# The second channel product of an attention and mixer kernel: its first block product is copied between PSUM banks by ScalarE, and the products come in another order

## The chip, the core and the metric

The kernel runs on one core of a Trainium2 chip. The metric is the device time of one execution in microseconds (us). Every time below is in us unless it is marked ns.

## What is computed

Eight batches of a gated attention unit without softmax, and behind it a token and channel mixer. All sizes are fixed: 3008 rows, 256 columns, 64 columns of `z`, 256 hidden token columns, 1536 hidden channel columns.

```python
scores = (z @ z.T) / 3008                 # per batch, 3008 x 3008
attn   = maximum(scores, 0) ** 2
x      = u * (attn @ v)                   # 3008 x 256
h      = maximum(x.T @ w_tok1, 0) @ w_tok2
u2     = x + h.T
h2     = maximum(u2 @ w_ch1, 0) @ w_ch2   # first and second channel product
out    = u2 + h2
```

The change is in the second channel product, `maximum(u2 @ w_ch1, 0) @ w_ch2`, alone.

## The kernel before

Work is tiled by blocks of 512 rows, six for each batch (`q` = 0 to 5; the last has 448). For each batch `b`, attention blocks come first; then the mixer of that batch: the first token product (`tok1`, L1058, tile `a_ps`), the second (`tok2`, L1128, tile `h_ps`), and for each block `q` the first channel product in six chunks (`ch1`, four matmuls of L1192 into tile `hp`, then a relu by ScalarE at L1231 into `h2pre`) and the second.

The second channel product uses a Strassen-like scheme with seven block products in place of eight. The hidden activations of a block of rows are seen as a 2 x 2 matrix of quarters (halves of the rows, even and odd hidden tiles), and so are the weights `w_ch2`. VectorE makes four sums of the quarters (`make_sums`, L1383, L1388, L1401, tile `hsum`), and mixes the weights once (`w_mix_sb`). A block product `k` is twelve matmuls of 128 columns (`product`, L1447; six where `q` = 5). After each product VectorE adds the 256 columns in PSUM to the output tile `ro` in SBUF (`collect` and its `add`, L1480; 128 columns where `q` = 5). Products that use the same sum go on accumulating in the same bank without being cleared: 1, then 6, 7 and 4 in the first bank of the tile `xb`; 5, then 3 in a bank of the tile `zb`; and product 2 alone in the other bank of `zb`. Products 1 and 2 belong to the same block of the output (columns 0 to 127 of the first half of the rows). So seven adds were needed for each `q`.

PSUM has eight banks; the kernel uses them as four pairs, or slots (`take_slot`, `bank_pair`). `xb`, `zb`, each `hp` chunk, the group tile `gp`, the attention accumulators and scores each take one while they live.

For `b` > 0 and `q` = 1 to 3 the first two of the six chunks are done in another scheme as four stages, written "a" to "d" (`grouped_ch1`, L1312, tile `gp`). Between the stages ScalarE copies one bank of `gp` to the other (`fork`, L1320) so that two accumulations can go on from one partial sum; it also copies a bank to SBUF (L1323), and takes the relus L1327 and L1331. VectorE adds two of the results at L1338.

The order of instructions on each engine is set when the program is built: a planner keeps a time for each engine, takes pieces off two lists (`heads` for token products, `tails` for channel products) when what they need is done by its own estimates, and gives the evacuations to the engines by priority (`first`). The order of pieces within `tails` is written by hand: `PLAIN` (before: a tuple without a name), `GROUPED` and `ORDER_LAST`, where a number is a block product, 0 stands for a `ch1` chunk of the next block (or, in `ORDER_LAST`, for what is left of `q` = 5 in the plain way, `ch2`, L1544) and a letter for a stage of `grouped_ch1` of the next block. There are 47 sets of seven products: every `(b, q)` but the very last, which is done by `ch2` alone. Of them 19 are in `PLAIN` order, 21 in `GROUPED` order, and 7, with `q` = 5, in `ORDER_LAST` order. The mixer of a batch and its attention do not mix piece by piece: the program has long stretches of one and of the other by turns, and the first token product of the next batch falls among the products of `q` = 5.

VectorE also makes the sums for the token product (`x_sums`, L926), the sums `t_sums` (L1268, L1273, L1278) for `grouped_ch1`, and gates and adds for attention. ScalarE does the relu of the scores (L496, L508) and copies accumulators (L825).

Of the kernel before, what the change touches and what calls it, by code (L numbers as in the profile page):

```python
# [14 lines left out]
P = 128  # L15
# [43 lines left out]
def kernel(  # L59
# [11 lines left out]
    nc = tc.nc  # L71
# [10 lines left out]
    NQ = (S + QW - 1) // QW  # L82
# [9 lines left out]
    first = ctx.enter_context(ExitStack())  # L92
# [276 lines left out]
    def push(engine, ready, busy, lat, fn, first=0, room=(), done=None, frees=()):  # L369
        op = Op(ready, busy, lat, fn, first, room, done, frees)  # L370
        waiting[engine].append(op)
        return op.done
# [577 lines left out]
    mix_done, tok_mix_done = Done(), Done()  # L950
# [70 lines left out]

    hid_done = Done()
    BORROW = 3
    GROUPED = ("a", 0, 1, 2, "b", 6, 5, 0, "c", 7, 3, 0, 4, "d")
    VERY_LAST = (B - 1, NQ - 1, CHT // 2 - 1)
    ORDER_LAST = ((1, 2, 6, 5, 7, 0, 3, 4), (1, 2, 6, 5, 0, 7, 3, 0, 4))

    def add_mixer(b):
        st = {}
# [141 lines left out]
        def with_u(q, ready, fn):  # L1171

            turned = st["turned", q].t
            if turned is None:
                st.setdefault(("waits", q), []).append(lambda t: fn(max(ready, t)))
            else:
                fn(max(ready, turned))
# [177 lines left out]
        def pairs_of(q):  # L1355

            return 2 if q < NQ - 1 else 1
# [56 lines left out]

        def bank_of(q, k):

            if k in (2, 5, 3):
                return st["zb", q][:, int(k != 2)]
            return st["xb", q][:, 0]

        def product(q, k, end):


            n = pairs_of(q)
            if k == 1:
                st["x_slot", q], _ = take_slot()
                st["xb", q] = bank_pair(st["x_slot", q], "xb")
            if k == 2:
                st["z_slot", q], _ = take_slot()
                st["zb", q] = bank_pair(st["z_slot", q], "zb")  # L1430
            to = bank_of(q, k)
            raw = {1: (0, 0), 2: (1, 0), 3: (1, 1)}
            mixed = {5: 0, 7: 1, 6: 2, 4: 3}
            w2 = w_ch2_sb.rearrange("p (j r) (h d) -> p j r h d", r=2, d=P)
            weights = {1: w2[:, :, 0, 0, :], 2: w2[:, :, 1, 0, :], 4: w2[:, :, 1, 1, :],
                       3: w_mix_sb[:, 3], 5: w_mix_sb[:, 0], 6: w_mix_sb[:, 1],
                       7: w_mix_sb[:, 2]}[k]
            first_use = k in (1, 2, 5)
            for c2 in range(CHT // 2):
                d, j = divmod(c2, 2)  # L1440
                for i in range(n):
                    if k in raw:
                        r, m = raw[k]
                        lhs = quarters(q, d)[:, r, m, j, i * P:(i + 1) * P]
                    else:
                        lhs = st["sum", q, d][:, mixed[k], j, i * P:(i + 1) * P]
                    nc.tensor.matmul(  # L1447
                        to[:, i * P:(i + 1) * P], lhs, weights[:, c2, :],
                        start=(first_use and c2 == 0 and i == 0), stop=(c2 == CHT // 2 - 1),
                        skip_group_check=True)  # L1450
            if k == 4:
                done_with_h2(q)
                for d in range(CHT // 4):
                    release(home_of(q), [1], end + 0.2)
            collect(q, k, end)

        def collect(q, k, end):


            n = pairs_of(q)  # L1460
            busy = 0.34 if n == 2 else 0.21
            source = bank_of(q, k)[:, :n * P].rearrange("p (i d) -> p i d", d=P)

            def res(m, h):
                return st["res", q][:, m * n:m * n + n, h * P:(h + 1) * P]

            def us(m, h):
                return st["u", q][:, h, m * n:m * n + n, :]

            blocks_of = {1: (0, 0), 2: (0, 0), 5: (1, 1), 6: (1, 0), 3: (1, 0), 7: (1, 1),  # L1470
                         4: (0, 1)}
            opening = k in (1, 5, 6, 4)

            def add(t):
                if k == 1:
                    home, n_home = take_home(q)
                    st["res", q] = sb.tile([P, QW // P, D], F32, tag=home, name="ro",
                                           bufs=n_home)
                m, h = blocks_of[k]
                nc.vector.tensor_add(  # L1480
                    res(m, h), source, us(m, h) if opening else res(m, h))
                recent[0] = st["res", q][:, 0, :1]
                over[q] -= 1
                if not over[q]:
                    nc.sync.dma_start(
                        out=rows_of(out[b], q)[:, :2 * n, :], in_=st["res", q][:, :2 * n, :])
                    free["sp"] = max(free["sp"], t) + 0.4
                    release(home_of(q), [1], t + 4.0)
                    release("us", us_uses[q])

            ready = end + 0.21
            done = taken[q, k]
            if k == 1:
                with_u(q, ready, lambda at: push(
                    "dve", at, busy, busy + 0.15, add, first=1, room=(home_of(q),),
                    frees=frees_of(q), done=done))
            else:
                done = push("dve", ready, busy, busy + 0.15, add, first=1, done=taken[q, k],
                            room=lambda: ("res", q) in st)
            if k == 3:  # L1500
                ring.append((done, st["z_slot", q]))
            if k == 4:
                ring.append((done, st["x_slot", q]))

        over = [7] * NQ
        us_uses = [[1] for _ in range(NQ)]
        s_done = {(q, d, k): Done() for q in range(NQ) for d in range(CHT // 4) for k in range(4)}
        taken = {(q, k): Done() for q in range(NQ) for k in range(1, 8)}
# [86 lines left out]
        for q in range(NQ):  # L1595
            heads.append(Piece(0.784, [x_done[b, NQ - 1], xd_done[b, q], tok_mix_done],
                               lambda end, q=q: tok1(q, end),
                               opens=q < NQ - 1, closes=q > 0, key=(b, 0), joins=q == 0 and b > 0))
        for q in range(NQ):
            heads.append(Piece(4 * column_time(widths[q]), [a_done[0], Sooner(a_done[1], 0.21), tok2_done[q]],  # L1600
                               lambda end, q=q: tok2(q, end), key=(b, 1)))
# [39 lines left out]
        def add_product(q, k):  # L1641
            needs = {
                1: [Sooner(h2_done[q, c], 0.111 * c) for c in range(CHT // 2)] + w_done[2:],
                2: [], 5: [mix_done, taken[q, 2]], 6: [taken[q, 1]], 3: [taken[q, 5]], 7: [taken[q, 6]],
                4: [taken[q, 7]]}[k]
            kind = {5: 0, 7: 1, 6: 2, 4: 3}.get(k)
            if kind is not None:
                needs = needs + [Sooner(s_done[q, d, kind], 0.222 * d) for d in range(CHT // 4)]
            if q == NQ - 1 and k == 5 and b % 2 == 0:
                needs = needs + [tok1_over[b + 1]]  # L1650
            cost = pairs_of(q) * (CHT // 2) * column_time(P)
            tails.append(Piece(cost, needs, lambda end: product(q, k, end), opens=k == 1,
                               closes=k == 4, key=(b, 2 + q), slot=k in (1, 2),
                               joins=k == 1 and q == NQ - 1))

        added = [0] * (NQ + 1)
# [6 lines left out]
        for q in range(NQ):  # L1663
            while added[q] < CHT // 2:
                add_next(q, q)
            if q + 1 < NQ and grouped(q + 1):
                added[q + 1] = 2
            rest = [(half, i) for half in halves(q) for i in range(pieces_of(q, half))]
            if fast(q):
                us_uses[q][0] += bool(rest)  # L1670
                h2_uses[q] += bool(rest)
                for k in (ORDER_LAST[b % 2] if q == NQ - 1 else GROUPED if grouped(q + 1) else
                          (0, 0, 1, 2, 0, 6, 5, 0, 7, 3, 0, 4)):
                    if isinstance(k, str):
                        add_grouped(q + 1, 0, "abcd".index(k), q)
                    elif k:
                        add_product(q, k)
                    elif rest:
                        add_ch2(q, *rest.pop(0))
                    elif b or q != HALF - 1 or added[q + 1] < BORROW:  # L1680
                        add_next(q + 1, q)
            else:
                for _ in range(2):
                    add_next(q + 1, q)
                for half, i in rest:
                    add_ch2(q, half, i)
# [259 lines left out]
    while cur[0] is not None or heads or tails:  # L1946
        run_engines(pe[0])
        ask_some()
        t = pe[0]
# [15 lines left out]
        n = can_score(done_units, most)  # L1965
        if n and blk is not None and blk.b == 1:
            b, q, _ = units[done_units][0]
            if b * NQ + q > NQ + blk.q + 1:
                n = 0
            if (b, q, blk.q) == (1, HALF, HALF - 1):  # L1970
                n = min(n, sum(u[0][:2] == (b, q) for u in units[:done_units]) < 2 * AHEAD)
# [118 lines left out]
```

## Time and profile before

| What | us |
|---|---|
| Three runs, median (lowest to highest) | 1109.5 (1109.03 to 1110.85) |
| The profiled execution | 1109.13 |
| Its span, first to last instruction | 1107.3 |

Busy time of the engines in the profiled execution:

| Engine | us | share of the span | instructions |
|---|---|---|---|
| PE (TensorE, matmuls) | 1102.2 | 100% | 11199 |
| PEld (weight loads) | 695.2 | 63% | 11199 |
| DVE (VectorE) | 811.5 | 73% | 1791 |
| ACT (ScalarE) | 684.7 | 62% | 906 |
| POOL (GpSimd) | 168.2 | 15% | 386 |

How to read it: an instruction row of the order in time has its start from the beginning of the span, the time it took (for several merged ones, from the first's start to the last's end), the engine, the line of the kernel, the operation, output tile and inputs, sizes, how many, and in brackets for how long the engine had been idle before and what ended that. A row of the groups has busy time, the mean of one in ns, and the idle time before. Matmuls overlap, so that the time each took says less than the distance of their starts. Line numbers are those of the kernel before.

### The profile page before, as it was taken

What the parts mean: (1) busy time and instruction counts of PE and PEld (TensorE: products, weight loads), DVE (VectorE), ACT (ScalarE), POOL (GpSimd) and SP (SyncE); (2) the same over time, 40 slices, a digit from 0 to 9 for tenths busy, and PEclk for the clock granted to TensorE, in tenths of its full rate; (3) what the DMA queues carried; (4) which work ended last, traced back from release to release, by engine and by line L of the source; (5) the groups of instructions that cost most, each with busy time, mean ns of one, the idle gap of its engine ahead of it and who ended that gap; (6) DMA issues with size and microseconds to landing.
All of it is one profiled execution on the core that took longest, in us unless ns stands there. A gap on an engine that the chain in (4) does not pass through costs nothing.

```text
span 1107.3 us, 27459 instructions
## 1 busy us (share of the span) xinstructions
PE 1102.2 (100%) x11199; PEld 695.2 (63%) x11199; DVE 811.5 (73%) x1791; ACT 684.7 (62%) x906; POOL 168.2 (15%) x386
## 2 busy tenths in 40 slices
PE   9999999999999999999999999999999999999998
PEld 3444575776557665576656865557755677556776
DVE  6889865886758866578766796567966778656785
ACT  7999555646854567546665467663776537743464
POOL 5320110321003110032100320003210120000100
PEclk9999999999999999999999999999999999999999
DMA  9999947798978969789896796977989778684222
GB/s 179 167 199 184 149 96 152 127 179 146 190 127 149 190 133 177 127 156 191 140 189 120 133 218 141 170 122 150 198 160 169 116 145 185 125 160 104 64 59 96
DMA packets 465726, 165.55 MB, mean 150 GB/s; under 512 B 433024, under 2 KB 448960, under 8 KB 465600
## 3 DMA queue, kind: packets, MB, share of 16 engines
q1 hardware_dynamic: 436208, 131.11, 58.9%
q0 software_dynamic: 28880, 32.32, 21.5%
q8 instruction: 87, 1.43, 0.6%
q14 instruction: 39, 0.32, 0.1%
q10 hardware_dynamic: 512, 0.38, 0.1%
HBM read 65.40 MB, written 24.64 MB: 81 GB/s over the span
## 4 chain that ended last, share of the span: by engine, by line
PE 99%; DVE 0%; ACT 0%; issue 0%
PE acc L697 42%; PE hp L1192 19%; PE xb L1447 11%; PE zb L1447 8%; PE sc L470 6%; PE h_ps L1128 4%; PE a_ps L1058 3%; PE gp L1312 3%; PE op L1544 2%; PE first_acc L614 1%; PE wp L210 0%; DVE at L516 0%; ACT at L508 0%; DVE zr L183 0%; PE first_acc L189 0%; DVE zT L1850 0%
## 5 line engine op out<-in xcount | busy, mean ns | idle before, releaser
L697 PEld LDWEIGHTS <-v_sb 64*128 64x128 bf16 x4418 | 245.7, 94 | 212.5 <-issue 1.3
L1231 ACT ACTIVATE h2pre<-hp 128x1024 bf16<-128x1024 f32 (+1 forms) x245 | 239.9, 1005 | 182.7 <-PE hp L1192 180.5
L697 PE MATMUL acc<-at,v_sb 64*128 64x512 bf16 (+1 forms) x2738 | 341.6, 374 | 0.0
L508 ACT ACTIVATE at<-sc 128x1024 bf16<-128x1024 f32 (+1 forms) x290 | 286.8, 1027 | 72.0 <-PE sc L470 66.4
L516 DVE TENSOR_TENSOR at<-at 128x1024 bf16<-128x1024 bf16 (+1 forms) x290 | 198.1, 687 | 112.1 <-ACT at L508 107.9
L1192 PE MATMUL hp<-xT,w_ch_sb 128*128 128x512 bf16 (+1 forms) x984 | 238.3, 374 | 0.0
L697 PE MATMUL acc<-fl,v_sb 64*128 64x512 bf16 (+1 forms) x1680 | 193.0, 367 | 0.0
L1192 PEld LDWEIGHTS <-w_ch_sb 128*128 128x128 bf16 x984 | 90.8, 98 | 79.0 <-issue 2.6
L1447 PEld LDWEIGHTS <-hsum 128*128 128x128 bf16 x2088 | 127.9, 98 | 19.6 <-issue 0.5
L470 PE MATMUL sc<-zT 64*128 64x512 bf16 (+1 forms) x732 | 132.4, 359 | 0.1
L1383 DVE TENSOR_TENSOR hsum<-h2pre 128x1024 bf16<-128x1024 bf16 (+1 forms) x141 | 90.0, 647 | 22.7 <-ACT h2pre L1231 12.6
L825 ACT COPY cp<-acc 128x512 f32<-128x512 f32 (+1 forms) x94 | 54.9, 584 | 79.9 <-PE acc L697 69.0
L831 DVE TENSOR_TENSOR cp<-acc,cp 128x512 f32<-128x512 f32 (+1 forms) x94 | 63.4, 675 | 54.8 <-ACT cp L825 54.0
L1447 PEld LDWEIGHTS <-h2pre 128*128 128x128 bf16 x1566 | 93.8, 98 | 10.0
L496 ACT ACTIVATE at<-sc 128x512 bf16<-128x512 f32 (+3 forms) x152 | 56.2, 450 | 29.2 <-PE sc L470 28.8
L1447 PE MATMUL xb<-shared_sb,hsum 128*128 128x128 bf16 x1044 | 73.6, 219 | 0.0
L1480 DVE TENSOR_TENSOR ro<-xb,u_sb 128x256 f32<-128x256 f32 (+1 forms) x141 | 56.3, 400 | 17.9 <-PE xb L1447 17.7
L470 PEld LDWEIGHTS <-zT 64*128 64x128 bf16 x732 | 42.4, 94 | 41.6 <-issue 3.8
L129 POOL CAST mark<-at 128x1 f32<-128x1 bf16 x24 | 9.3, 386 | 388.1 <-DVE at L516 388.1
L851 DVE TENSOR_TENSOR xT<-cp,uT 128x512 bf16<-128x512 f32 (+1 forms) x94 | 62.4, 663 | 0.8
L547 DVE TENSOR_TENSOR at<-at 128x512 bf16<-128x512 bf16 (+3 forms) x152 | 41.0, 320 | 23.8 <-ACT at L496 23.8
L1401 DVE TENSOR_TENSOR hsum<-h2pre,hsum 128x512 bf16<-128x512 bf16 (+1 forms) x141 | 55.1, 400 | 4.1 <-ACT h2pre L1331 2.5
(107 smaller groups left out, 1114.8 us busy)
## 6 DMA issues: line engine op xcount, KB each, us to landing
out_dram<-ro SPq DMA_DIRECT2D x40, 512.0 KB, 3.2
v_sb<-in_v_dram POOLq DMA_DIRECT2D x40, 256.0 KB, 4.6
ur<-in_u_dram POOLq DMA_DIRECT2D x40, 256.0 KB, 5.0
w_tok_sb<-in_moe_w_tok_dram POOLq DMA_DIRECT2D x10, 256.0 KB, 10.5
shared_sb<-in_z_dram POOLq DMA_DIRECT2D x35, 64.0 KB, 4.2
at<-at SPq DMA_TRANSPOSE x114, 2.4
out_dram<-ro SPq DMA_DIRECT2D x7, 256.0 KB, 3.7
fl<-at SPq DMA_TRANSPOSE x105, 4.5
```

The source lines that it names most:

```text
L470: nc.tensor.matmul(sc[:, r, c0:c1], zT[h, k:k + P], zT[h, m + c0:m + c1], start=True, stop=True)
L496: nc.scalar.activation(a3[:, i, c0:c1], sc[:, r, c0:c1], ACT.Relu, scale=inv_S)
L508: nc.scalar.activation(view, sv, ACT.Relu, scale=inv_S)
L516: nc.vector.tensor_mul(view, view, view)
L697: nc.tensor.matmul(o, vs[blk.b, g][rows, i, dh * P:(dh + 1) * P], rhs, start=(dh, h) not in blk.begun, stop=stop, skip_group_check=True)
L831: nc.vector.tensor_add(cp[:, :W], acc[:, 0, :W], cp[:, :W])
L851: nc.vector.tensor_mul(xT[:, dh, :full * P].rearrange("p (t s) -> p t s", s=P), acc[:, :full * P].rearrange("p (t s) -> p t s", s=P), uT[: ...
L1192: nc.tensor.matmul(hps[r % len(hps)][:, r, :W], w_ch1_sb[:, dc, cc * P:(cc + 1) * P], xT[:, dc, :W], start=(dc == 0), stop=(dc == DT - 1))
L1231: nc.scalar.activation(h2[:, :, :W], hp[:, :, :W], ACT.Relu)
L1383: nc.vector.tensor_sub(sums["s"][:, 0:2, :, :n * P], h[:, :, 1], h[:, 0])
L1447: nc.tensor.matmul(to[:, i * P:(i + 1) * P], lhs, weights[:, c2, :], start=(first_use and c2 == 0 and i == 0), stop=(c2 == CHT // 2 - 1), ...
L1480: nc.vector.tensor_add(res(m, h), source, us(m, h) if opening else res(m, h))
```

## The change

Product 1 is no longer added to the output by VectorE. In its place ScalarE copies its bank of `xb` (256 columns, or 128 where `q` = 5) into the second bank of `xb`, and product 2 accumulates on that copy without clearing it, while 6, 7 and 4 go on in the first bank as before. One add then takes in products 1 and 2 together. It is now the first add, the one that creates the output tile. `zb` holds only products 5 and 3, in its first bank, and its slot is taken at product 5 in place of product 2. Product 2 waits for the copy, product 6 too, and product 4 waits for product 2's add. All three orders of products change.

```diff
     BORROW = 3
-    GROUPED = ("a", 0, 1, 2, "b", 6, 5, 0, "c", 7, 3, 0, 4, "d")
+    FIRST = 2
+    GROUPED = ('a', 0, 1, 0, 'b', 6, 2, 5, 'c', 7, 0, 3, 4, 'd')
+    PLAIN = (0, 1, 0, 5, 2, 6, 0, 0, 7, 0, 3, 4)
     VERY_LAST = (B - 1, NQ - 1, CHT // 2 - 1)
-    ORDER_LAST = ((1, 2, 6, 5, 7, 0, 3, 4), (1, 2, 6, 5, 0, 7, 3, 0, 4))
+    ORDER_LAST = ((1, 2, 6, 5, 0, 7, 3, 4), (1, 2, 5, 6, 0, 3, 7, 0, 4))
...
         def bank_of(q, k):
 
-            if k in (2, 5, 3):
-                return st["zb", q][:, int(k != 2)]
-            return st["xb", q][:, 0]
+            if k in (5, 3):
+                return st["zb", q][:, 0]
+            return st["xb", q][:, int(k == 2)]
...
-            if k == 2:
+            if k == 5:
                 st["z_slot", q], _ = take_slot()
                 st["zb", q] = bank_pair(st["z_slot", q], "zb")
...
-            first_use = k in (1, 2, 5)
+            first_use = k in (1, 5)
...
-            blocks_of = {1: (0, 0), 2: (0, 0), 5: (1, 1), 6: (1, 0), 3: (1, 0), 7: (1, 1),
-                         4: (0, 1)}
-            opening = k in (1, 5, 6, 4)
+            blocks_of = {2: (0, 0), 5: (1, 1), 6: (1, 0), 3: (1, 0), 7: (1, 1), 4: (0, 1)}
+            opening = k in (2, 5, 6, 4)
+
+            def fork(t):
+                nc.scalar.copy(bank_of(q, 2)[:, :n * P], bank_of(q, 1)[:, :n * P])
 
             def add(t):
-                if k == 1:
+                if k == FIRST:
...
             if k == 1:
+                push("act", ready, busy, busy + 0.15, fork, first=2, done=done)
+            elif k == FIRST:
                 with_u(q, ready, lambda at: push(
...
-        over = [7] * NQ
+        over = [6] * NQ
...
-                2: [], 5: [mix_done, taken[q, 2]], 6: [taken[q, 1]], 3: [taken[q, 5]], 7: [taken[q, 6]],
-                4: [taken[q, 7]]}[k]
+                2: [taken[q, 1]], 5: [mix_done], 6: [taken[q, 1]], 3: [taken[q, 5]], 7: [taken[q, 6]],
+                4: [taken[q, 7], taken[q, 2]]}[k]
...
-                               closes=k == 4, key=(b, 2 + q), slot=k in (1, 2),
+                               closes=k == 4, key=(b, 2 + q), slot=k in (1, 5),
...
                 for k in (ORDER_LAST[b % 2] if q == NQ - 1 else GROUPED if grouped(q + 1) else
-                          (0, 0, 1, 2, 0, 6, 5, 0, 7, 3, 0, 4)):
+                          PLAIN):
```

## The prediction

> **What bounds the kernel now.** I read the engine table of the page first, then its chain, then the windows, then the order in time of two product sets. In the page:
>
> ```profile
> span 1107.3 us, 27459 instructions
> PE 1102.2 (100%) x11199; PEld 695.2 (63%) x11199; DVE 811.5 (73%) x1791; ACT 684.7 (62%) x906; POOL 168.2 (15%) x386
> PE 99%; DVE 0%; ACT 0%; issue 0%
> ```
>
> TensorE (PE) has something in flight during the whole span and carries 99% of the chain that ends last; VectorE (DVE) and ScalarE (ACT) have a quarter and more than a third of the span to spare. The windows say the same of the steady part and of the mixer of the last batch, the only one that no attention work of a next batch follows:
>
> ```profile
> core 0: us, PE busy (x) PEld busy (x) DVE busy (x) ACT busy (x) POOL busy (x), PEclk, DMA share, GB/s
> 40.00:1100.00 1060.00, 1059.87 (x10899) 675.18 (x10894) 780.27 (x1739) 650.98 (x869) 150.98 (x349) 1.00 0.81 149
> 1011.00:1098.00 87.00, 86.94 (x965) 64.11 (x962) 67.82 (x167) 49.46 (x60) 3.28 (x9) 1.00 0.26 66
> ```
>
> Busy TensorE is not yet TensorE at its pace, since matmuls overlap; the pace is read from starts. One set of seven products with `PLAIN` order begins so (before: a chunk of the first channel product is 4 matmuls of L1192, a block product 12 of L1447):
>
> ```profile
> 1078.43 2.75 PE L1192 MATMUL hp<-xT,w_ch_sb 128*128 128x512 bf16 x12
> 1081.02 0.83 PE L1447 MATMUL xb<-w_ch_sb,h2pre 128*128 128x128 bf16 x12
> 1081.69 0.83 PE L1447 MATMUL zb<-w_ch_sb,h2pre 128*128 128x128 bf16 x12
> 1082.36 1.03 PE L1192 MATMUL hp<-xT,w_ch_sb 128*128 128x512 bf16 x4
> 1083.22 0.83 PE L1447 MATMUL xb<-shared_sb,hsum 128*128 128x128 bf16 x12
> ```
>
> Three chunks take 2.59, so 0.86 each; a product takes 0.67, or 56 ns for a matmul of 128 columns, at a granted clock of 1.00. Each starts as the one ahead of it stops issuing. The time is therefore the matmuls' own issue time, and a change to ACT and DVE can only add waits, or take away the few that are left. One that is left shows where a wait comes from:
>
> ```profile
> 1092.02 0.92 PE L1192 MATMUL hp<-xT,w_ch_sb 128*128 128x448 bf16 x4
> 1092.97 0.83 PE L1447 MATMUL xb<-shared_sb,hsum 128*128 128x128 bf16 x12
> 1097.83 0.92 PE L1192 MATMUL hp<-xT,w_ch_sb 128*128 128x448 bf16 x4
> 1098.59 0.27 PE L1544 MATMUL op<-w_ch_sb,h2pre 128*128 128x256 bf16 x1
> 1092.50 0.42 DVE L1480 TENSOR_TENSOR ro<-xb,u_sb 128x256 f32<-128x256 f32 x1
> ```
>
> A 448-wide chunk takes 0.76 (1097.83 to 1098.59), but here product 6 (L1447, 1092.97) starts 0.95 after it: 0.2 lost, until the add of product 1 has read the bank (1092.50 + 0.42 = 1092.92). So from the end of an evacuation to the matmul that waits for it I take 0.05.
>
> **What the change removes and adds.** The built program keeps every matmul (11,200) and, between two stretches of attention, the same number of pieces of each kind; the switches between half-array and full-array work stay as many. It has 47 VectorE instructions fewer and 47 ScalarE instructions more, one for each product set (19 `PLAIN`, 21 `GROUPED`, 7 `ORDER_LAST`; 40 of 256 columns, 7 of 128). DMAs and POOL's instructions stay in number. Prices:
>
> ```profile
> L1480 DVE TENSOR_TENSOR ro<-zb,ro 128x256 f32<-128x256 f32 (+1 forms) x94 | 37.4, 398 | 3.4 <-PE zb L1447 2.7 <-POOL mark L129 0.3
> L1320 ACT COPY gp<-gp 128x512 f32<-128x512 f32 x42 | 23.9, 570 | 1.3
> L1078 ACT COPY a_f<-a_ps 128x128 f32<-128x128 f32 x8 | 2.1, 265 | 33.7 <-PE a_ps L1058 33.7
> ```
>
> The adds give back 47 x 0.398 = 18.7 us of VectorE. The copy of 256 columns does not occur before; it lies between 0.265 (128 columns) and 0.570 (512), 0.37 on the straight line, which I take since both ends are copies from PSUM by the same engine. That is 40 x 0.37 + 7 x 0.265 = 16.7 us more ScalarE. Neither is on the chain: cover is TensorE's own work, and what matters is the margin at each new wait. If a cover were gone, the price would be the missing part of it times the sets.
>
> **`PLAIN` sets**, counted from the start of the last chunk of this 512-row block (t = 0). The new order on TensorE is: last chunk, chunk, P1, chunk, P5, P2, P6, two chunks, P7, chunk, P3, P4; so P1 starts at 1.73, P5 at 3.26, P2 at 3.93, P6 at 4.60, P7 at 7.00, P4 at 9.20. ScalarE and VectorE in the trace, t = 0 at 1078.43, and two adds in a row from another set:
>
> ```profile
> 1079.49 2.85 ACT L1231 ACTIVATE h2pre<-hp 128x1024 bf16<-128x1024 f32 x3 [0.24 <-PE hp L1192]
> 1080.55 0.69 DVE L1383 TENSOR_TENSOR hsum<-h2pre 128x1024 bf16<-128x1024 bf16 x1 [0.15 <-ACT h2pre L1231]
> 255.85 0.41 DVE L1480 TENSOR_TENSOR ro<-xb,ro 128x256 f32<-128x256 f32 x1
> 256.18 0.41 DVE L1480 TENSOR_TENSOR ro<-zb,ro 128x256 f32<-128x256 f32 x1
> ```
>
> The last chunk's evacuation starts at 1.06 (0.20 after its matmuls) and ends at 2.1 (the sum that waits for it starts at 1080.55, 2.12); three take 2.85, so they follow each other by 0.92.
> - P1 moves up by a chunk. Its eleventh matmul, at 1.73 + 10 x 0.056 = 2.29, is the first to need that evacuation: margin 0.15. Where the second chunk is 448 wide (8 sets) P1 comes 0.10 sooner and the margin is 0.05. I count nothing for the first and 0.2 in all for the second (0 to 0.4).
> - The copy is queued behind the second evacuation (1.98, next start 2.90), ready at 2.60: it runs 2.90 to 3.27. P2 at 3.93 has 0.6. Behind it on ScalarE waits the third chunk's evacuation, ready only at 3.46.
> - P5 needs the first sum at 3.71; it ends at 2.81.
> - P6 needs the copy alone. The built program lets P2's add wait for the end of P6 (5.27): adds of P2, P5, P6 then start at 5.47, 5.81, 6.15 (0.33 apart, as at 255.85 and 256.18) and end at 6.57; P7 at 7.00 has 0.4.
>
> **`GROUPED` sets**, t = 0 at 247.83:
>
> ```profile
> 247.83 1.03 PE L1192 MATMUL hp<-xT,w_ch_sb 128*128 128x512 bf16 x4
> 248.69 0.38 PE L1312 MATMUL gp<-xT,w_ch_sb 128*128 128x256 bf16 x2
> 249.13 1.03 PE L1192 MATMUL hp<-xT,w_ch_sb 128*128 128x512 bf16 x4
> 249.81 0.58 ACT L1323 COPY s<-gp 128x512 f32<-128x512 f32 x1
> 250.42 0.57 ACT L1320 COPY gp<-gp 128x512 f32<-128x512 f32 x1
> 250.91 1.03 ACT L1231 ACTIVATE h2pre<-hp 128x1024 bf16<-128x1024 f32 x1
> 252.03 0.60 ACT L1327 ACTIVATE h2pre<-gp 128x512 bf16<-128x512 f32 x1
> 251.35 0.42 DVE L1401 TENSOR_TENSOR hsum<-h2pre,hsum 128x512 bf16<-128x512 bf16 x1
> 253.65 0.42 DVE L1268 TENSOR_TENSOR t_sums<-xT 128x512 bf16<-128x512 bf16 x1
> 254.71 1.23 DVE L1338 CUSTOM_DVE_ANT_1 h2pre<-gp,s 128x1024 bf16<-128x1024 f32 x1 [0.31 <-PE gp L1312]
> 256.61 0.83 PE L1447 MATMUL xb<-w_ch_sb,hsum 128*128 128x128 bf16 x12
> ```
>
> A group stage of four matmuls takes 0.44 (248.69 to 249.13). New starts: P1 2.16, b 3.70, P6 4.13, P2 4.80, P5 5.47, c 6.14, P7 6.58, chunk 7.25, P3 8.12, P4 8.79. ScalarE: copies of the group 1.98 and 2.59 to 3.16, the new copy 3.1 to 3.5, evacuation to 4.5, the group's relu and copy 4.5 to 5.6, evacuation 5.5 to 6.5. So b has 0.5, P6 0.6, c 0.5 and the chunk at 7.25 0.7 to spare. VectorE: P2's add creates the output tile and now comes before P6's, at 5.67; P6's is at 6.00 to 6.42, so P7 at 6.58 has 0.1: the tightest of all. P7's own add follows the 1.23 us of L1338 (6.78) at about 7.9 and ends at 8.35, 0.4 ahead of P4 (in the trace 255.85 + 0.41 = 256.26, and P4 at 256.61).
>
> **`ORDER_LAST` sets** put 14 matmuls (0.78) of the next batch's first token product between P1 and P2; the copy (0.20 + 0.265 + 0.05) has 0.26.
>
> **Waits that I do count.** After attention the mixer starts with
>
> ```profile
> 335.15 2.76 PE L1192 MATMUL hp<-xT,w_ch_sb 128*128 128x512 bf16 x12
> 336.01 0.53 ACT L825 COPY cp<-acc 128x448 f32<-128x448 f32 x1 [1.74 <-DVE xT L856]
> 336.44 2.86 ACT L1231 ACTIVATE h2pre<-hp 128x1024 bf16<-128x1024 f32 x3
> 162.17 0.42 DVE L1480 TENSOR_TENSOR ro<-xb,u_sb 128x256 f32<-128x256 f32 x1 [1.07 <-PE xb L1447]
> 162.65 0.83 PE L1447 MATMUL xb<-shared_sb,hsum 128*128 128x128 bf16 x12
> ```
>
> There the accumulator's copy (336.01) delays the first evacuation to 336.44, so it ends at about 337.46; P1's eleventh matmul would be due at 335.15 + 2.29 = 337.44. 0.1 lost, at seven such starts: +0.7. And where batch 0's mixer breaks off for attention only one chunk lies between P6 and P7: the adds end 1.29 after P6, P7 is due at 0.86, so +0.5 once (before, the add of 162.17 ended 0.06 ahead of P7). With +0.2 from the 448-wide sets and -0.2 for the wait at 1092.97, the sum is +1.2.
>
> The profiled execution took 1109.13 us, 0.4 under the median of the three (1109.5; its span is 1107.3). 1109.13 + 1.2 = 1110.3; with part of that 0.4 the forecast is 1110.5. About 0.2%, or 2.2 us, is what a measurement of this kernel can tell from no change, so this is no change.
>
> **Rivals.**
> - Slower: VectorE reaches the new first add late. In `GROUPED` sets P7 then waits for P6's add, which stands behind P2's. It decides from the point where P2's add starts later than 5.8; one sum of 0.42 in front of it costs 0.3 in each, 21 x 0.3 = 6.3, or 1115.8. For it: the margin is 0.1. Against: VectorE's last sum ends at 3.9 (251.35 + 0.42), and the three `t_sums`, which now follow it and take 0.42 at most each, end by 5.2. 0.14.
> - Slower: the copy stands behind one more evacuation (0.92) than I read. P2 of a `PLAIN` set then waits 0.3: 19 x 0.3 = 5.7, or 1115.2. The built order has the copy ahead of it. 0.06.
> - Faster: TensorE is not at its limit, since its weight loads fill only 675.18 of 1060, and VectorE's 47 adds, 0.33 apart, come off the time: -15.5, or 1094. Against it stand the 56 ns of every product matmul and no gap between pieces. 0.02. The Trainium skill (Perfetto Trace Analysis, Identifying the Most-Contended Engine) judges TensorE's headroom by weight-load share and not by matmul busy time, which would leave a third free here; the starts of this trace speak against that reading.
> - That the change does nothing of what it says is out: the 47 copies stand in the built program.
>
> **Numbers.** Forecast 0.78; slower 0.14 + 0.06 = 0.20; faster 0.02; same 0.78. The low end is the sum without any new wait, less the spread of the executions (1109.03): 1108.6. The high end doubles the counted waits and adds a tenth to P7 in the 21 grouped sets (+1.2 + 2.1, from 1110.3): 1113.4.
>
> **What would show it.** Right: TensorE at 99% of the chain, P1 to P4 0.67 each, VectorE near 793 us, ScalarE near 701, no wait over 0.2 in product sets save the one of 0.5 in batch 0. Wrong: a gap ahead of P7 or P2 that repeats in each set, or TensorE's starts closer than 56 ns for 128 columns.

## The result, and the profile after

| | before | after |
|---|---|---|
| median (lowest to highest) of nine runs each | 1109.23 (1108.88 to 1112.08) | 1111.96 (1111.19 to 1114.88) |
| the profiled execution; its span | 1109.13; 1107.3 | 1111.98; 1110.2 |

The ratio is 1.0023, with a 95% interval of 1.0014 to 1.0032: the changed kernel is about 2.6 us slower. That lies in the forecast range (1108.6 to 1113.4) and 1.5 above the forecast of 1110.5; the middle of the interval is just past the 0.2% that I called no change, and its lower end is below it.

From the page of the changed kernel, its span, its engines and its chain:

```profile
span 1110.2 us, 27434 instructions
PE 1103.2 (99%) x11199; PEld 695.3 (63%) x11199; DVE 801.1 (72%) x1744; ACT 698.2 (63%) x953; POOL 163.1 (15%) x386
PE 96%; DVE 1%; DMA 1%; ACT 1%; issue 0%; POOL 0%; DVEq 0%; ACTq 0%; SPq 0%; POOLq 0%
```

The 47 copies have come, the 47 adds have gone, and TensorE still carries the chain, though 96% of it and not 99%. New in the third line are the one per cents of VectorE, a DMA and ScalarE: the chain now passes through them behind places where TensorE waits. These shares count the whole stretch of work behind a wait; TensorE itself lost far less, as listed below. The copies, by shape, in the groups of the changed kernel (busy time, mean ns, idle time before):

```profile
L1476 ACT COPY xb<-xb 128x256 f32<-128x256 f32 x40 | 15.3, 381 | 0.0
L1476 ACT COPY xb<-xb 128x128 f32<-128x128 f32 x7 | 1.8, 250 | 2.6 <-PE xb L1449 2.6
```

A copy of 256 columns takes 0.381, against the 0.37 that I took; together they take 17.1, against 16.7.

To find where the 2.9 us of span went, I listed each matmul that starts later than the columns of the one ahead of it allow, from 100 us on and where the wait is over 0.08. Gaps of one missing matmul record are left out, and so is the 0.1 at the first matmul of each attention stretch, which stands eight times in either kernel. Four long waits stand in the changed kernel at places where the kernel before has none. The rows below are its order in time, with PE, DVE, ACT and SP rows of one place side by side; the brackets name what ended the wait. Line numbers are now those of the kernel whose rows are shown: in the changed one a product is L1449, an add L1484, a chunk L1194.

The first is where batch 0's mixer breaks off (product 6, a chunk, product 7; the adds of products 2 and 6):

```profile
160.97 0.83 PE L1449 MATMUL xb<-shared_sb,hsum 128*128 128x128 bf16 x12
161.64 1.03 PE L1194 MATMUL hp<-xT,w_ch_sb 128*128 128x512 bf16 x4
161.90 0.42 DVE L1484 TENSOR_TENSOR ro<-xb,u_sb 128x256 f32<-128x256 f32 x1 [1.80 <-PE xb L1449]
162.57 0.41 DVE L1484 TENSOR_TENSOR ro<-xb,u_sb 128x256 f32<-128x256 f32 x1
163.04 0.83 PE L1449 MATMUL xb<-shared_sb,hsum 128*128 128x128 bf16 x12 [0.37 <-DVE ro L1484]
```

Product 7 was due at 161.64 + 0.86 = 162.50 and starts at 163.04, 0.06 after the last of three adds: 0.54. The first add starts 0.26 after product 6 stops issuing (161.64), though product 2, whose result it reads, had stopped issuing one product earlier.

The second is the restart of that mixer after attention:

```profile
201.37 2.87 ACT L1233 ACTIVATE h2pre<-hp 128x1024 bf16<-128x1024 f32 x3
202.20 0.72 PE L1449 MATMUL xb<-w_ch_sb,h2pre 128*128 128x128 bf16 x10
203.37 0.29 PE L1449 MATMUL xb<-w_ch_sb,h2pre 128*128 128x128 bf16 x2 [0.45 <-ACT h2pre L1233]
```

Product 1 runs ten of its matmuls (202.20 to 202.76) and waits 0.62 for the second of these three evacuations before the eleventh. The evacuations are late from the start of this stretch, and were so in the kernel before, where product 1 came later in the order and did not feel it. There the mixer starts at 198.34, and:

```profile
199.63 0.53 ACT L825 COPY cp<-acc 128x448 f32<-128x448 f32 x1 [0.60 <-DVE xT L856]
200.06 4.70 ACT L1231 ACTIVATE h2pre<-hp 128x1024 bf16<-128x1024 f32 x5
```

The first evacuation starts 1.72 after the mixer. At 335.15, the one start that I had read for all seven, it was 1.29, and 1.10 to 1.28 at the five after it. The third wait is that of product 7 of the set `q` = 4 in batch 0:

```profile
211.90 0.34 SPq L1489 DMA_DIRECT2D out_dram<-ro  x1
216.03 1.68 PE L1194 MATMUL hp<-xT,w_ch_sb 128*128 128x448 bf16 x8
217.29 0.42 DVE L1484 TENSOR_TENSOR ro<-xb,u_sb 128x256 f32<-128x256 f32 x1 [1.37 <-DMA out_dram<-ro]
217.96 0.41 DVE L1484 TENSOR_TENSOR ro<-xb,u_sb 128x256 f32<-128x256 f32 x1
218.43 0.38 PE L1449 MATMUL xb<-shared_sb,hsum 128*128 128x128 bf16 x4 [0.72 <-DVE ro L1484]
```

Two 448-wide chunks end their issue at 217.54; product 7 starts at 218.43, 0.89 late. The first add could have started at about 216.25 (0.2 after product 6's end at 216.03) and starts at 217.29: VectorE waited 1.37 for an output DMA, that of the block before, issued at 211.90. The fourth is product 5 of the last 512-row set:

```profile
1091.96 1.83 ACT L1233 ACTIVATE h2pre<-hp 128x1024 bf16<-128x1024 f32 x2 [1.18 <-PE hp L1194]
1093.83 0.20 DVE L1207 COPY hs<-h2pre 128x128 bf16<-128x128 bf16 x1 [2.30 <-ACT h2pre L1233]
1093.93 0.69 DVE L1385 TENSOR_TENSOR hsum<-h2pre 128x1024 bf16<-128x1024 bf16 x1
1093.94 1.13 PE L1449 MATMUL zb<-shared_sb,hsum 128*128 128x128 bf16 x12
```

Its twelve matmuls take 1.13 and not 0.83. The sum that they read is queued on VectorE behind a copy of the batch's last rows (L1207) that waits for the next block's evacuation, which ends at 1091.96 + 1.83 = 1093.79. The same copy and sum stand behind the 0.2 of product 6 at 1092.97 in the kernel before, which I had booked as a gain. There they held up the add of product 1 (1092.50):

```profile
1091.23 0.20 DVE L1205 COPY hs<-h2pre 128x128 bf16<-128x128 bf16 x1 [2.30 <-ACT h2pre L1231]
1091.34 0.68 DVE L1383 TENSOR_TENSOR hsum<-h2pre 128x1024 bf16<-128x1024 bf16 x1
```

Two more waits stand in this one execution: 0.63 in product 1 at 339.9 and 0.17 in product 7 at 761.6. New waits are 0.54 + 0.62 + 0.89 + 0.29 + 0.63 + 0.17 = 3.1; gone are the 0.2 at 1092.97 and three of 0.1 ahead of product 6 or 4. The difference, 2.6, is close to the 2.9 by which the span grew. Another 0.2 ahead of the second token product (L1128, L1130 after) is in neither sum: it stands three times in the kernel before and four times in the changed one.

### The profile page after: what moved, and what is told of

Read it like the earlier page. It is cut to its first block, busy times and chain, and to the rows that moved or that the text cites. A ratio compares the mean times of both kernels' runs of the same rounds, so it can differ in the third digit from the quotient of the medians.

```text
span 1110.2 us, 27434 instructions
## 1 busy us (share of the span) xinstructions
PE 1103.2 (99%) x11199; PEld 695.3 (63%) x11199; DVE 801.1 (72%) x1744; ACT 698.2 (63%) x953; POOL 163.1 (15%) x386
## 4 chain that ended last, share of the span: by engine, by line
PE 96%; DVE 1%; DMA 1%; ACT 1%; issue 0%; POOL 0%; DVEq 0%; ACTq 0%; SPq 0%; POOLq 0%
PE acc L697 41%; PE hp L1194 18%; PE xb L1449 13%; PE sc L470 6%; PE zb L1449 5%; PE h_ps L1130 4%; PE a_ps L1060 3%; PE gp L1314 3%; PE op L1550 2%; PE first_acc L614 1%; DMA x_pair<-xT 1%; DMA out_dram<-ro 0%; ACT at L508 0%; DVE ro L1484 0%; ACT h2pre L1233 0%
## 5 line engine op out<-in xcount | busy, mean ns | idle before, releaser
L1194 PE MATMUL hp<-xT,w_ch_sb 128*128 128x512 bf16 (+1 forms) x984 | 238.6, 374 | 0.0
L1194 PEld LDWEIGHTS <-w_ch_sb 128*128 128x128 bf16 x984 | 90.7, 98 | 78.8 <-issue 2.6
L1449 PEld LDWEIGHTS <-hsum 128*128 128x128 bf16 x2088 | 128.2, 98 | 12.7 <-issue 1.9
L1449 PEld LDWEIGHTS <-h2pre 128*128 128x128 bf16 x1566 | 97.0, 98 | 20.0 <-ACT h2pre L1233 1.3
L1385 DVE TENSOR_TENSOR hsum<-h2pre 128x1024 bf16<-128x1024 bf16 (+1 forms) x141 | 90.1, 648 | 20.7 <-ACT h2pre L1233 18.9
L825 ACT COPY cp<-acc 128x512 f32<-128x512 f32 (+1 forms) x94 | 54.9, 584 | 78.6 <-PE acc L697 67.5
L1484 DVE TENSOR_TENSOR ro<-xb,u_sb 128x256 f32<-128x256 f32 (+1 forms) x141 | 54.5, 399 | 42.1 <-PE xb L1449 39.2
L1449 PE MATMUL xb<-w_ch_sb,h2pre 128*128 128x128 bf16 x1044 | 74.9, 219 | 0.9 <-ACT h2pre L1233 0.9
L1449 PE MATMUL xb<-shared_sb,hsum 128*128 128x128 bf16 x1044 | 73.7, 219 | 1.1 <-DVE ro L1484 1.1
```

Source lines behind the costliest of these rows:

```text
L825: nc.scalar.copy(cp[:, :W], acc[:, 1, :W])
L1194: nc.tensor.matmul(hps[r % len(hps)][:, r, :W], w_ch1_sb[:, dc, cc * P:(cc + 1) * P], xT[:, dc, :W], start=(dc == 0), stop=(dc == DT - 1))
L1385: nc.vector.tensor_sub(sums["s"][:, 0:2, :, :n * P], h[:, :, 1], h[:, 0])
L1449: nc.tensor.matmul(to[:, i * P:(i + 1) * P], lhs, weights[:, c2, :], start=(first_use and c2 == 0 and i == 0), stop=(c2 == CHT // 2 - 1), ...
```

## The experiments

Every kernel was timed against the kernel before on the same chip, and its waits listed from its own profile in the same way.

**The changed kernel once more.**

> The changed kernel once more, unchanged. Theory W (the waits of single places cost the time): the profile shows the same four long waits as the first profile of it, within 0.15 us each: ahead of product 7 where batch 0's mixer breaks off (0.54, at 163.0), inside product 1 at the starts of batch 0's second and batch 1's first mixer stretch (0.62 at 203.4, 0.63 at 339.9), ahead of product 7 in the set q = 4 of batch 0 (0.89 at 218.4); ratio to the kernel before 1.0015 to 1.003. Rival R (run to run jitter): the long waits lie elsewhere or are gone, ratio under 1.0015.

1112.05, ratio 1.0024 (1.0015 to 1.0033). 0.54, 0.62, 0.93 and 0.29 are there again; the 0.63 at 339.9 is not (0.08 there), and product 7 waits 0.29 at 896.4 instead of 0.17 at 761.6. So theory W holds for three of the four waits that it lists, and 0.29 is fixed too. The rest change from run to run, 339.9 among them, which I had listed with the fixed ones. The copy of the accumulator on ScalarE, in after and then in the repeat, shows what varies:

```profile
336.56 0.42 DVE L926 TENSOR_TENSOR d_pair<-x_pair 128x512 bf16<-128x512 bf16 x1 [0.47 <-DMA x_pair<-xT]
338.41 0.53 ACT L825 COPY cp<-acc 128x448 f32<-128x448 f32 x1 [2.29 <-DVE xT L856]
```

```profile
338.00 0.53 ACT L825 COPY cp<-acc 128x448 f32<-128x448 f32 x1 [1.74 <-DVE xT L856]
895.30 0.42 DVE L1484 TENSOR_TENSOR ro<-xb,u_sb 128x256 f32<-128x256 f32 x1 [1.10 <-DMA out_dram<-ro]
```

In after, VectorE waited 0.47 for a transposing DMA, so the copy at L825 and the evacuations behind it came later, 1.41 after the mixer's start against 0.86 in the repeat, which has no such wait. The last row is the wait at 896.4: an output DMA again.

**Two chunks ahead of product 1.**

```diff
-    PLAIN = (0, 1, 0, 5, 2, 6, 0, 0, 7, 0, 3, 4)
+    PLAIN = (0, 0, 1, 5, 0, 2, 6, 0, 3, 7, 0, 4)
```

> Only the order of the plain sets is changed: two chunks ahead of product 1 again, product 5 directly behind it, and product 3 and a chunk between 6 and 7. Theory W: the waits inside product 1 at the mixer starts go (0.6 each at two starts), and product 7 in the q = 4 set and at batch 0's break-off has a product more ahead of it (0.67), so both of its waits fall below 0.25; 1109.5 to 1110.5, 1.5 to 2.4 below the changed kernel. Rival C (the 13 us more of ScalarE cost the time wherever the copies stand): 1111.5 to 1112.5 as the changed kernel.

1119.02, ratio 1.0088 (1.0074 to 1.0101): a miss for both theories. Product 1 at the restart waits no more, as expected (product 2 there waits 0.17 for its copy), but product 3 of the plain sets now waits, 0.2 to 1.1, and in some product 4. One place:

```profile
494.50 0.42 DVE L1484 TENSOR_TENSOR ro<-xb,u_sb 128x256 f32<-128x256 f32 x1 [1.35 <-PE xb L1449]
494.84 0.41 DVE L1484 TENSOR_TENSOR ro<-zb,u_sb 128x256 f32<-128x256 f32 x1
495.31 0.83 PE L1449 MATMUL zb<-shared_sb,h2pre 128*128 128x128 bf16 x12 [0.24 <-DVE ro L1484]
```

Product 3 continues on product 5's bank and needs product 5's add. That add stands behind product 2's, which creates the output tile and starts only after product 6. A product put into the gap to hide a wait had a wait of its own.

**The copy alone, in the orders of before.** All three orders are those of the kernel before.

> The copy alone: the orders of the kernel before, with product 2 right behind product 1 in the 40 sets of 256 columns. Theory W: product 2 waits for the copy in each of the 40; in a plain set the copy stands behind an evacuation, 1.0 us (ready 3.46, evacuation to 3.82, copy 0.39, 0.05, against a start due at 3.26), in a grouped set behind the group's two copies, up to 1.55; 19 x 1.0 + 21 x 1.55 = 52 at most, less what other waits had anyway: 1140 to 1162. Rival H (TensorE's queue or the planner hides the copy in any order): 1109 to 1113.

1154.10, ratio 1.0403 (1.0389 to 1.0417), as W had it, and rival H is out. A plain set:

```profile
151.54 0.40 ACT L1476 COPY xb<-xb 128x256 f32<-128x256 f32 x1
151.98 0.83 PE L1449 MATMUL xb<-w_ch_sb,h2pre 128*128 128x128 bf16 x12 [0.82 <-ACT xb L1476]
```

Product 2 starts 0.04 after the copy ends, about 1.0 late (1.2 in the first plain set of later batches). In grouped sets it is 0.66 to 0.77 late, about half of the 1.55 that I gave as the most. The 40 waits of product 2 add up to 35.4. Product 6 waits another 9.0 in 32 sets, 0.3 in each grouped one, for VectorE's add of product 2. Together this is the 44.5 by which the kernel is slower.

**The orders alone, with seven adds and no copy.**

> The orders alone: the kernel before, with its seven adds and no copy, in the three new orders. Theory W: the waits inside product 1 at the mixer starts and the wait of product 7 at batch 0's break-off stay (0.6, 0.6, 0.5), the wait of 0.89 in the q = 4 set of batch 0 goes, since the first add is product 1's again and its output tile is made earlier: 1110.5 to 1111.5. Rival C (ScalarE's copies cost the time): as the kernel before, 1109.0 to 1109.6. Rival V (the 47 adds more on VectorE make product 7 late in each grouped set, whose margin I took as 0.1): 21 x 0.3, 1115 to 1118.

1118.76, ratio 1.0090 (1.0076 to 1.0104): W's forecast fell, C is out, and V comes nearest in size (1115 to 1118) but names the wrong product. It is product 4 of two of the three grouped sets of most batches that waits, 0.38 and 0.5:

```profile
394.69 1.22 DVE L1339 CUSTOM_DVE_ANT_1 h2pre<-gp,s 128x1024 bf16<-128x1024 f32 x1
395.82 0.42 DVE L1484 TENSOR_TENSOR ro<-xb,ro 128x256 f32<-128x256 f32 x1
396.29 0.83 PE L1451 MATMUL xb<-w_ch_sb,hsum 128*128 128x128 bf16 x12 [0.39 <-DVE ro L1484]
```

Product 7's add stands behind the 1.22 of the group's sum, and with one add more ahead of that sum it is too late for product 4. The wait at the restart (0.62) is there too, so the order makes it and not the copy; the 0.54 at the break-off is not there, so that one belongs to the shared tile `xb`. The 0.89 in the set `q` = 4 of batch 0, which I expected to go, stays, now behind a sum:

```profile
217.05 0.42 DVE L1384 TENSOR_TENSOR hsum<-h2pre 128x512 bf16<-128x512 bf16 x1 [1.10 <-DMA out_dram<-ro]
217.39 0.42 DVE L1484 TENSOR_TENSOR ro<-xb,u_sb 128x256 f32<-128x256 f32 x1
```

The output tile is made early here, at product 1's add, and it is the next tile, that of the sum, which waits for the output DMA of the block before; product 6's add (217.39) and product 7 wait behind it. In the kernel before a sum waits at this place too, 0.43 for that DMA (L1383 at 215.57), with product 6's add behind it, but that add still starts at 215.91, in time for product 7 at 216.52. The two halves of the change cost 9.2 and 44.5 us by themselves, against 2.6 together: each needs the other.

**Products 2 and 5 change places.**

```diff
-    PLAIN = (0, 1, 0, 5, 2, 6, 0, 0, 7, 0, 3, 4)
+    PLAIN = (0, 1, 0, 2, 5, 6, 0, 0, 7, 0, 3, 4)
```

> Products 2 and 5 change places in the plain order, nothing else. Theory T (products 2 and 6 write two banks of one tile, and the add of product 2, issued after product 6, waits for the end of product 6; so three adds bunch ahead of product 7): now product 5 stands between 2 and 6, the add of product 2 starts 0.2 after product 2's end, only one add follows product 6, and the wait of 0.54 ahead of product 7 at batch 0's break-off falls to 0.1 or less; the wait of 0.29 in product 5 at 1094.7 goes too. Against it product 2 is due 0.67 sooner and may wait up to 0.1 for the copy, in 19 sets: 1110.9 to 1113. Rival B (VectorE is simply busy there): the 0.54 stays.

1116.76, ratio 1.0068 (1.0056 to 1.0080). The mechanism of T shows, and the time does not. First the adds of 2 and 6 at the break-off, then the add of 2 and product 6 at a later place:

```profile
161.23 0.42 DVE L1484 TENSOR_TENSOR ro<-xb,u_sb 128x256 f32<-128x256 f32 x1 [0.53 <-PE xb L1449]
162.57 0.42 DVE L1484 TENSOR_TENSOR ro<-xb,u_sb 128x256 f32<-128x256 f32 x1 [0.31 <-PE xb L1449]
341.74 0.42 DVE L1484 TENSOR_TENSOR ro<-xb,u_sb 128x256 f32<-128x256 f32 x1
342.22 0.83 PE L1449 MATMUL xb<-shared_sb,hsum 128*128 128x128 bf16 x12 [0.33 <-DVE ro L1484]
```

The add of product 2 no longer waits for product 6, one add alone follows that product, and the 0.54 is gone. But the tie works the other way too: product 6, which writes the other bank of the tile, now waits for product 2's add, 0.5 to 0.6 in each later batch, and product 2 waits about 0.2 for the copy.

**The output tile taken at the copy.** In `fork`, and so as early as product 1's add took it before:

```diff
             def fork(t):
+                home, n_home = take_home(q)
+                st["home", q] = sb.tile([P, QW // P, D], F32, tag=home, name="ro",
+                                        bufs=n_home)
                 nc.scalar.copy(bank_of(q, 2)[:, :n * P], bank_of(q, 1)[:, :n * P])
...
                 if k == FIRST:
-                    home, n_home = take_home(q)
-                    st["res", q] = sb.tile([P, QW // P, D], F32, tag=home, name="ro",
-                                           bufs=n_home)
+                    st["res", q] = st["home", q]
```

> The output tile is taken when the copy is made, as early as the kernel before took it at the add of product 1; the adds stay. Theory D (the 0.9 ahead of product 7 at 218.5 comes from the first add, which in the changed kernel got the buffer that the output DMA of the block before was still reading): the wait at 218.5 goes, to 0.1 or less, the others (0.54 at 163, 0.62 at 203.4, 0.29 at 1094.6) stay: 0.9 less than the changed kernel, 1110.9 to 1111.4. Rival B (the adds' queue on VectorE): it stays, 1112.

1110.55, ratio 1.0016 (1.0004 to 1.0028): 1.4 us less than the changed kernel. What D says of the wait holds, and the time is below the 1110.9 that it gave as the least. The 0.89 is gone (the first add, the sum that comes next on VectorE, and product 7 of that set):

```profile
216.11 0.42 DVE L1485 TENSOR_TENSOR ro<-xb,u_sb 128x256 f32<-128x256 f32 x1 [1.33 <-PE xb L1449]
217.12 0.43 DVE L1385 TENSOR_TENSOR hsum<-h2pre 128x512 bf16<-128x512 bf16 x1
217.37 0.83 PE L1449 MATMUL xb<-shared_sb,hsum 128*128 128x128 bf16 x12
```

In the list of what VectorE waited for ahead of the adds (us, times), after has

```profile
  DMA out_dram<-ro: 1.9, 3
```

and this kernel has none of it. The waits at 761.6 and 896.4 were of the same kind and are gone too, which is a part of why more than 0.9 came back; two new waits of 0.14 ahead of product 4 stand against it. The built programs show the reason: in the changed kernel the output tile of that set gets the very buffer of the block before, whose output DMA has just been issued; in the kernel before and in this one it gets a buffer that a sum had freed long ago. The buffer of the block before then goes to the next sum, here as in the seven adds without a copy. Here that sum (217.12) stands behind the three adds in VectorE's order and holds up none of them; there it stood ahead of product 6's add. So it takes both, the early tile and this place of the sum.

**The copy on VectorE.**

```diff
-                nc.scalar.copy(bank_of(q, 2)[:, :n * P], bank_of(q, 1)[:, :n * P])
+                nc.vector.tensor_copy(bank_of(q, 2)[:, :n * P], bank_of(q, 1)[:, :n * P])
...
-                push("act", ready, busy, busy + 0.15, fork, first=2, done=done)
+                push("dve", ready, busy, busy + 0.15, fork, first=2, done=done)
```

> The copies are made by VectorE, so that it has seven operations a set as before. Theory W (VectorE's room in the grouped sets is what the copy on ScalarE buys): product 4 or 7 of the grouped sets waits 0.3 to 0.5 in most of the 21, and product 2 of a few sets for the copy: 1117 to 1123. Rival E (which engine copies does not matter since TensorE sets the time): 1111.5 to 1112.5.

1114.86, ratio 1.0050 (1.0038 to 1.0062), 2.9 above the changed kernel: E is out, and W is too high and has the wrong place. No product of a grouped set waits over 0.15. The added waits are those of product 7 in sets `q` = 4 (1.04, 0.67, 0.49, 0.32, 0.31), and three more of 0.2 ahead of the second token product. A copy takes 0.43 there:

```profile
L1476 DVE COPY xb<-xb 128x256 f32<-128x256 f32 x40 | 17.1, 426 | 0.1
```

**Each copy twice.** A second copy, the same as the first, right behind it.

> Every copy is made twice, 15 to 17 us more ScalarE. Theory M (margins: product 2 has 0.6 to spare in a plain set, more in a grouped one, 0.26 against 0.27 where q = 5): as the changed kernel, 1111.5 to 1113. Rival C (ScalarE's load itself costs time, about 2.6 us for the first 13.5): another 2.5 to 3, 1114.5 to 1115.5.

1112.72, ratio 1.0029 (1.0017 to 1.0041): M holds, C's 2.5 did not come. The group of copies has doubled to

```profile
L1477 ACT COPY xb<-xb 128x256 f32<-128x256 f32 x80 | 29.5, 369 | 1.3
```

and product 2 waits for none of them. The 0.8 above the changed kernel is in product 7 of the `q` = 4 sets again (0.14 to 0.55 in four of them, and 1.16 for 0.89 at 218.6).

**Three repairs.** The early tile, and two sets of batch 0 with orders of their own:

```diff
+    BREAK_OFF = (0, 1, 0, 2, 5, 6, 0, 7, 3, 4)
+    RESTART = (0, 0, 1, 0, 5, 2, 6, 0, 0, 7, 3, 4)
...
-                          PLAIN):
+                          BREAK_OFF if (b, q) == (0, HALF - 1) else
+                          RESTART if (b, q) == (0, HALF) else PLAIN):
```

> The early output tile as in the run before, and two sets of batch 0 get orders of their own: where the mixer breaks off, product 2 ahead of product 5 (three chunks as before); where it starts again, two chunks ahead of product 1 and the chunk behind product 7 gone. Theory S (the single waits add up to the whole difference): the 0.54 at 163 and the 0.62 at 203 go, to 0.15 or less each, only the 0.29 near 1093 and small waits of single runs are left; 1.0 less than with the early tile alone, 1109.4 to 1109.8, within 0.05% of the kernel before. Rival C (the copies keep a cost of their own): 1110.3 or more.

1110.53, ratio 1.0011 (1.0002 to 1.0020). The 0.54 and the 0.62 are gone, but the time is not better than with the early tile alone: product 2 of the restart waits 0.21, and product 4, without a chunk ahead of product 3, waits 0.75:

```profile
209.09 0.68 DVE L1387 TENSOR_TENSOR hsum<-h2pre 128x1024 bf16<-128x1024 bf16 x1
209.69 0.41 DVE L1487 TENSOR_TENSOR ro<-xb,ro 128x256 f32<-128x256 f32 x1
210.16 0.72 PE L1451 MATMUL xb<-w_ch_sb,hsum 128*128 128x128 bf16 x10 [0.58 <-DVE ro L1487]
```

A sum stands ahead of product 7's add in VectorE's order. By its time this run is in the range of rival C; by its waits it is S with two new ones, 0.96 together, that my own order added. The next run tells the two apart.

**The break-off alone, and another restart.** First the early tile with `BREAK_OFF` alone:

> Early output tile and the break-off order alone; the restart keeps the plain order. Theory S (single waits add up): the 0.54 at 163 is gone and nothing comes in its place, the 0.62 at 203 and the 0.29 at 1093 stay: 0.5 below the early tile alone (1110.55), 1109.9 to 1110.2, and the profiled execution 0.7 to 1.0 above that of the kernel before. Rival C (the copies keep a cost of their own beside these waits): 1110.5 or more.

1109.85, ratio 1.0008 (0.9998 to 1.0018). As S has it (0.05 under its range), and clear of rival C's 1110.5: of the long waits only the 0.62 and the 0.29 are left, and product 7 follows its chunk almost at once (add of 6, chunk, product 7):

```profile
161.95 1.03 PE L1195 MATMUL hp<-xT,w_ch_sb 128*128 128x512 bf16 x4
162.15 0.42 DVE L1486 TENSOR_TENSOR ro<-xb,u_sb 128x256 f32<-128x256 f32 x1 [0.31 <-PE xb L1450]
162.81 0.83 PE L1450 MATMUL xb<-shared_sb,hsum 128*128 128x128 bf16 x12
```

Then the three repairs with `RESTART = (0, 0, 1, 0, 5, 2, 6, 0, 7, 0, 3, 4)`:

> As the run with three repairs, but at the restart the chunk stands between products 7 and 3 and only one chunk between 6 and 7. Theory S: product 4 has its chunk again, so its wait of 0.75 goes; the adds of 2, 5 and 6 end 1.28 after product 6 and product 7 is due at 0.86, so it waits 0.4 (0.2 for product 2 stays): 0.35 below the run with three repairs, 1110.0 to 1110.3. Rival A (VectorE has room there after all): no wait over 0.2, 1109.6 to 1109.8.

1109.97, ratio 1.0006 (0.9997 to 1.0015). Product 4's wait went, product 7 waits 0.55 (expected 0.4) for the third add of a row, and product 2 keeps its 0.21; rival A is out. So of the orders tried here, each costs the restart 0.6 to 1.0. These last two kernels can't be told from the kernel before, and none of the variants beats it.

The sums of all waits over 0.08, listed as above and without those ahead of the second token product, stand beside the profiled executions:

| Kernel | waits | time |
|---|---|---|
| before | 2.2 | 1109.13 |
| early tile and break-off | 2.9 | 1109.94 |
| with the other restart | 3.2 | 1109.80 |
| three repairs | 3.3 | 1110.04 |
| early tile | 3.4 | 1110.04 |
| after, repeated | 4.3 | 1111.69 |
| after | 4.8 | 1111.98 |
| each copy twice | 5.6 | 1112.66 |

Against the kernel before, times and sums differ alike, within 0.5. About 1.7 us of each sum are in every kernel: 0.1 each where TensorE changes from attention to the token products and the mixer, and inside product 1 of the seven sets `q` = 5.

## Why the prediction was right, and where it was short

**TensorE's own issue as the bound: right.** 99% busy, the same pace, 47 VectorE instructions fewer without a gain. The rival at 1094 is out. What moved the time were single gaps between TensorE's matmuls. The Trainium skill (Perfetto Trace Analysis, Identifying the Most-Contended Engine) judges TensorE by weight-load share and by MFU, the share of the peak FLOP/s. The weight loads' share is 63% in both kernels, and reading a third of TensorE as free from it does not hold for this kernel; MFU was not worked out. The Trainium skill (Perfetto Trace Analysis, Optimization Strategy) also tells one to look for gaps on the engine that one optimizes, and this case agrees.

**The copy at nothing: right.** 0.381 measured for 0.37, no wait of product 2 in a plain set, and doubling the copy left product 2 without one. In the orders of before it would have cost 44.5.

**Product 7 in the grouped sets, margin 0.1: right, and it held.** Two adds and product 7 of one set:

```profile
255.41 0.76 DVE L1484 TENSOR_TENSOR ro<-xb,u_sb 128x256 f32<-128x256 f32 x2 [1.01 <-PE xb L1449]
256.26 0.83 PE L1449 MATMUL xb<-shared_sb,hsum 128*128 128x128 bf16 x12
```

Product 6's add ends at 256.17, and product 7 starts 0.09 later, in its place; the first rival, 1115.8, did not come. All 21 sets have this 0.09. Nor did the second rival come: in the `PLAIN` set that starts at 1081.03 the copy runs from 2.88 after the start, where I had 2.90.

**The counted waits.** The break-off: +0.5 expected, 0.54 measured, and the tie of product 2's add to product 6 is its cause, since it goes where the two are parted. The seven starts: +0.7 expected as 0.1 each, and 0.75 measured in the repeat, but as 0.62 at one start and 0.02 to 0.08 at three. That the sum came out is luck: I had read one start for all seven, and the 0.62 is the one start at which the first evacuation comes 1.72 after the mixer's and not 1.1 to 1.3. The 448-wide sets: +0.2 expected in product 1, nothing measured there. The wait at 1092.97: -0.2 expected and gone, but its cause, the sum behind a copy on VectorE, was not; it came back as 0.29 in product 5.

**The step that fell short** is the margin of product 7 in `PLAIN` sets. I set the adds to start 0.2 after product 6 and gave product 7 0.4 to spare, which is what the set at 1081.03 shows. In sets `q` = 4 the first add waited for its output buffer, and product 7 lost 0.9 in batch 0 and 0.2 to 0.3 in one more set of each execution. I had written that the add which creates the output tile moves from product 1 to product 2, and costed its place in VectorE's queue, not the buffer that it takes there. With the tile taken early the time fell by 1.4, and what is then left above the kernel before, 1.1 (1110.55 against 1109.43 on that chip), is about the +1.2 of the sum, in part by luck again: it holds the 0.29 and the two waits of 0.14 that I had not counted, in place of starts that cost nothing.

My own signs of being right were not all met. I wrote that no wait over 0.2 would stand in product sets but the 0.5 of batch 0, and there are four more: 0.62, 0.89, 0.63 and 0.29. TensorE has 96% of the chain and not 99%. So the time lies in the range by the range's width, and in part for other reasons than those counted. By its own terms (1110.3 + 1.2 + 2.1) the high end would have been 1113.6 and not 1113.4; nothing hangs on that.

VectorE's busy time fell by 10.4 where I had 18.7. The durations of its instructions, added up singly, fell by 18.9 (906.7 to 887.8 in the two traces), as forecast. But busy time counts an overlap once: adds in a row start 0.33 apart and take 0.41, and in the changed kernel the overlaps on VectorE are 8.5 fewer us in all.

## What to carry to other kernels

On an engine that is full, a change of its helpers is judged place by place: a margin worked out for the typical set says little of the sets at the edges of a stretch, where work stops, restarts or a buffer is short. An instruction that takes a buffer and is moved later takes another buffer, perhaps one whose DMA has just been issued; the place where the tile is taken can be kept when the instruction moves. And in this program two banks in one tile are one thing for the waits, in both directions: a read of one bank was held for a write to the other, and where the order was turned, the write was held for the read.

## What was not expected of the hardware

- The same program's execution differs in single waits: where a transposing DMA landed 0.47 too late for VectorE, TensorE lost 0.63 in product 1, and 0.08 in the execution in which it was not late. The nine runs of that kernel lie within 0.4% of each other.
- ScalarE's copy of 256 columns from one PSUM bank to another took 0.381, VectorE's 0.426; the ScalarE copy of 128 columns took 0.250.
